# Attention with a squared-ReLU MLP behind it: q and k of six batches transposed by DMA instead of by TensorE

## The chip, the cores and the metric

One core of one Trainium2 chip runs the whole program. The metric is the device time of one execution in microseconds (us); a kernel is known by the median of its timed runs. The profile is of one further execution, whose own time stands beside its span. TensorE is PE in the profile (PEld its weight loads), VectorE is DVE, ScalarE is ACT, GpSimd is POOL and SyncE is SP; SP and POOL issue the DMAs.

## What is computed

```python
# q, k, v: (8, 12, 448, 64) fp32; w_in: (768, 2048); w_out: (2048, 768)
scores = (q @ k.transpose(0, 1, 3, 2)) / sqrt(64)
m = scores.max(-1, keepdims=True)
e = exp(scores - m)
attn = e / (e.sum(-1, keepdims=True) + exp(-m) + 1e-9)   # softmax with one more, empty, key
x = (attn @ v).transpose(0, 2, 1, 3).reshape(3584, 768)
out = maximum(x @ w_in, 0) ** 2 @ w_out                   # (3584, 768) fp32
```

The kernel leaves the maximum out: `exp(s) / (sum exp(s) + 1)` is the same quotient.

## The kernel before

**Pairs.** There are 8 batches of 12 heads. The unit of attention is a pair of heads, so 6 pairs a batch and 48 in all; one turn of the main loop (L251) works on one pair. The 448 tokens of a head lie on 112 partitions, four successive tokens to a partition (`P`, `RUN`), so the tokens fall into four groups `kk` of 112.

**q and k.** `load` (L78) brings q, k and v of a batch from DRAM through POOL's queue, which casts fp32 to fp16 on the way (tiles `qn`, `kn`, `vn`, two buffers each). For the first three pairs of batch 0 `load_raw` (L86) brings q and k as fp32 through SP's queue. The scores need the 64 dimensions of a head on partitions, so q and k are transposed: `regroup` (L102) has DVE copy three pairs at a time into `flatq` and `flatk`; `transposes` (L114) has PE make, for one pair, four transposes of `flatq` and four of `flatk` into one PSUM tile `mp`; DVE copies that to `qkt` (L121). In `qkt` the first head of the pair is on partitions 0 to 63, the second on 64 to 127.

**Scores and values.** `scores` (L124) makes, for one group `kk` of keys, two matmuls (one a head, 64 rows of the array each, 448 columns) into `sp`, and ACT takes the exponential into `et` (L129). `values` (L138) multiplies with v, `row_sums` (L144) adds up over the keys, ACT makes the reciprocal as `exp(-ln(z))`, and `normalise` (L154) writes the pair's columns of `xt`.

**MLP.** `mlp` (L161) is a generator: for a block of 384 (even batches) or 512 (odd batches) tokens it makes 16 times six matmuls with `win` into `mp` (L167), each followed on DVE by a maximum (L172) and a square (L174), and then 16 matmuls with `wout` for each half row of 128 tokens (L182), which ACT copies to `ot` (L186) and SP stores (L196). `drain` (L233) runs the generator for a share of its time at five places in a turn, so that the matmuls of the block of the batch before fill PE between the steps of attention. A batch's first turn still drains the end of the block before that one. The block of batch 7 runs alone at the end.

**Order.** Each engine works through its instructions in the order in which the program issues them. In a turn for pair i: scores of groups 0 and 1; transposes of pair i+1; MLP; scores of group 2; scores of group 3; values and row sums of pair i-1; MLP, with the three sums over `et` on DVE (L133, L136) between; normalise of pair i-1; and at the end of a turn with pr 1 the regroup of the same batch's pairs 3 to 5, with pr 4 that of the next batch's pairs 0 to 2. `mp` has two buffers in PSUM, shared by the transposes and the MLP; `sp` has two, `ot` two.

**Loads.** POOL's queue at the start: v of batch 0 (half), q and k of its pairs 3 to 5, the rest of v, three eighths of `win`, half of batch 1, three more eighths, the other half, the last two, four quarters of `wout`. Later a batch b+1 is loaded when turn (b, 0) is issued, as soon as the buffers are free.

Of the kernel before, what the change touches and what calls it, by code (L numbers as in the profile page):

```python
# [15 lines left out]
def kernel(  # L16
# [18 lines left out]
    P = S // RUN  # L35

# [34 lines left out]
    nats, flats, xts = {}, {}, {}  # L71

    def tiles_of(b):
        if b not in nats:
            nats[b] = {n: nat.tile([P, H, RUN, D], FP16, name=f"{n}n") for n in ("q", "k", "v")}
        return nats[b]

    def load(b, names, p0, p1):  # L78
        hs = slice(2 * p0, 2 * p1)
        for n in names:  # L80
            r = {"q": q_r, "k": k_r, "v": v_r}[n]
            nc.gpsimd.dma_start(out=tiles_of(b)[n][:, hs], in_=r[b, :, hs])  # L82

    raws = {}

    def load_raw(b, p0, p1):  # L86
        hs = slice(2 * p0, 2 * p1)
        for n, r in (("q", q_r), ("k", k_r)):
            t = raw.tile([P, 2 * (p1 - p0), RUN, D], FP32, name=f"{n}raw{p0}")
            nc.sync.dma_start(out=t, in_=r[b, :, hs])  # L90
            raws[n, b, p0] = t
# [10 lines left out]
    def regroup(b, p0, p1):  # L102
        hs = slice(2 * p0, 2 * p1)
        n = 2 * (p1 - p0)
        both = []
        for name in ("q", "k"):
            t = raws.pop((name, b, p0)) if (name, b, p0) in raws else nats[b][name][:, hs]
            f = flat.tile([P, RUN, H // 2, D], FP16, name=f"flat{name}")
            nc.vector.tensor_copy(f[:, :, 0:n, :], t.rearrange("p h t d -> p t h d"))  # L109
            both.append(f)  # L110
        for pr in range(p0, p1):
            flats[b, pr] = both, 2 * (pr - p0)

    def transposes(b, pr):  # L114
        both, h0 = flats.pop((b, pr))
        tp = m_psum.tile([128, 2, 512], FP16, name="mp")
        for i, t in enumerate(both):
            for s in range(RUN):
                nc.tensor.transpose(tp[:, i, P * s:P * s + P], t[:, s, h0:h0 + 2, :], ident[0:P, 0:P])  # L119
        qkt = qkt_pool.tile([128, 2, S], FP16, name="qkt")  # L120
        nc.vector.tensor_copy(qkt, tp[:, :, 0:S])  # L121
        return qkt

    def scores(qkt, et, kk):  # L124
        sp = s_psum.tile([P, 2, 512], FP32, name="sp")
        for h in range(2):
            r = slice(64 * h, 64 * h + 64)
            nc.tensor.matmul(sp[:, h, 0:S], qkt[r, 1, P * kk:P * kk + P], qkt[r, 0, :], start=True, stop=True)  # L128
# [8 lines left out]

    def values(b, pr, et, xp, kk):  # L138
        vn = nats[b]["v"]
        for h in range(2):  # L140
            nc.tensor.matmul(xp[64 * h:64 * h + 64, 0:S], vn[:, 2 * pr + h, kk, :], et[:, kk, h, :],  # L141
                             start=(kk == 0), stop=(kk == RUN - 1))

    def row_sums(es):  # L144
        zp = xz_psum.tile([128, 512], FP32, name="zp")
        for h in range(2):
            nc.tensor.matmul(zp[64 * h:64 * h + 64, 0:S], ones, es[:, 0, h, :], start=True, stop=True)  # L147
# [13 lines left out]
    def mlp(t0, n):  # L161
# [15 lines left out]
        for ts in range(n // 128):  # L177
# [13 lines left out]
            while c < end:  # L191
                b, t, p = c // S, c % S // P, c % P
                m = min(P - p, end - c)
                o = c + 128 - end
                rows = out[b * S:(b + 1) * S, :].rearrange("(p t) m -> t p m", t=RUN)
# [3 lines left out]


    load_raw(0, 0, 1)
    load_raw(0, 1, 3)
    load(0, "v", 0, 3)
    load(0, "qk", 3, 6)
    load(0, "v", 3, 6)
# [6 lines left out]
    for i in range(3):  # L212
        load_win(i, 8)
    load(1, "qkv", 0, 3)
# [114 lines left out]
```

## Time and profile before

| | us |
|---|---|
| median of 3 runs | 496.74 (496.45 to 499.69) |
| the profiled execution | 497.45 |
| its span, first to last instruction | 495.7 |
| PE busy in it | 448.1 |
| DVE busy in it | 280.8 |
| ACT busy in it | 244.2 |
| mean granted TensorE clock | 0.978 |

The span leaves 1.7 us of the execution around it. The turn of one batch after the other is seen at ACT's first reciprocal step (`lnz`, L150), once a pair: the second turns of batches 1 to 7 have it at 54.34, 109.13, 170.29, 225.08, 286.24, 341.07 and 403.13 us, and the last one stands at 446.09 us; from there to the end the block of batch 7 runs alone. In the views, a line of the timeline gives the start, the busy time, engine, line, tiles, shapes, how many are merged in it (x4), and in brackets how long the engine sat idle before it and what ended that. Busy time of PE includes the depth of its pipeline, so matmuls that are started 50 ns apart are shown as 200 ns each: the starts tell the pace.

### The profile page before, as it was taken

How to read it: one execution, taken by the hardware profiler on the slowest of the kernel's cores; microseconds unless marked ns; L12 is line 12 of the kernel's file. 1: busy time of each engine (PE TensorE's matmuls, PEld its weight loads, DVE VectorE, ACT ScalarE, POOL GpSimd, SP SyncE). 2: the span in 40 equal slices, each digit the busy share in tenths (PEclk: the TensorE clock that was granted, in tenths of full speed). 3: DMA queues.
4: the chain of work that ended last, by engine and by line, in shares of the span. 5: the costliest groups of instructions: out<-in, count | busy, mean ns of one | idle time of the engine just before them, and what ended most of it. 6: DMA issues, size and time to landing. Idle time of an engine off the chain costs nothing.

```text
span 495.7 us, 7052 instructions
## 1 busy us (share of the span) xinstructions
PE 448.1 (90%) x2912; PEld 221.9 (45%) x2912; DVE 280.8 (57%) x532; ACT 244.2 (49%) x345; POOL 35.5 (7%) x46
## 2 busy tenths in 40 slices
PE   1787789997999979997999988998999989999996
PEld 1333345543355534543355534553345544455453
DVE  2656766457853568457754466637684277635800
ACT  2688436663355635663365635565245663561011
POOL 6342100001000010001000010000000000000000
PEclk9998999999999989999999989999899998999999
DMA  9999990256112580144702545115001210021022
GB/s 184 197 197 206 205 184 7 65 87 86 26 33 65 88 110 3 33 68 66 99 1 64 79 79 75 34 32 89 0 2 33 63 33 0 1 65 32 1 62 67
DMA packets 45665, 34.97 MB, mean 71 GB/s; under 512 B 1600, under 2 KB 42048, under 8 KB 45632
## 3 DMA queue, kind: packets, MB, share of 16 engines
q0 software_dynamic: 39744, 22.12, 33.1%
q1 hardware_dynamic: 5888, 12.39, 8.5%
q8 instruction: 23, 0.38, 0.3%
q14 instruction: 10, 0.08, 0.0%
HBM read 45.61 MB, written 11.01 MB: 114 GB/s over the span
## 4 chain that ended last, share of the span: by engine, by line
PE 73%; DVE 20%; ACT 3%; DMA 2%; issue 1%; SPq 0%; ACTq 0%
PE mp L182 30%; PE mp L167 20%; PE xp L141 9%; PE sp L128 8%; DVE rt L172 6%; PE mp L119 4%; DVE es L133 4%; DVE g L174 4%; DMA kraw<-in_k_dram 2%; PE zp L147 2%; DVE xt L158 2%; ACT et L129 2%; DVE es L136 2%; DVE qkt L121 2%; DVE flatq L109 1%
## 5 line engine op out<-in xcount | busy, mean ns | idle before, releaser
L129 ACT ACTIVATE et<-sp 112x896 f16<-112x896 f32 x192 | 165.3, 913 | 167.9 <-PE sp L128 167.9
L167 PE MATMUL mp<-xt,win 128*128 128x384 f16 (+1 forms) x768 | 163.6, 363 | 6.5 <-DVE rt L172 3.5
L182 PE MATMUL mp<-wout,g 128*128 128x512 f16 (+1 forms) x896 | 153.9, 326 | 0.4
L167 PEld LDWEIGHTS <-win 128*128 128x128 f16 x768 | 74.5, 100 | 86.2 <-issue 27.9
L182 PEld LDWEIGHTS <-g 128*128 128x128 f16 x896 | 84.9, 98 | 61.0 <-issue 9.2
L172 DVE TENSOR_SCALAR rt<-mp 128x384 f16<-128x384 f32 (+1 forms) x128 | 79.6, 622 | 56.4 <-PE mp L167 53.2
L133 DVE TENSOR_TENSOR es<-et 112x896 f16<-112x896 f16 x96 | 59.1, 622 | 83.0 <-ACT et L129 82.8
L128 PE MATMUL sp<-qkt 64*112 64x448 f16 x384 | 62.3, 395 | 4.3 <-ACT et L129 3.6
L186 ACT ACTIVATE ot<-mp 128x512 f32<-128x512 f32 (+1 forms) x56 | 27.3, 487 | 72.8 <-PE mp L182 72.1
L174 DVE TENSOR_TENSOR g<-rt 128x384 f16<-128x384 f16 (+1 forms) x128 | 50.1, 392 | 4.4
L141 PE MATMUL xp<-et,vn 112*64 112x448 f16 x384 | 49.7, 377 | 0.0
L121 DVE COPY qkt<-mp 128x896 f16<-128x896 f16 x48 | 29.8, 621 | 32.3 <-PE mp L119 32.3
L119 PE MATMUL mp<-ident,flatq 112*128 112x112 f16 x192 | 19.0, 226 | 28.9 <-DVE flatq L109 20.6
L128 PEld LDWEIGHTS <-qkt 64*112 64x112 f16 x384 | 19.2, 130 | 42.3 <-issue 40.0
L150 ACT ACTIVATE lnz<-zp,one_b 128x448 f32<-128x448 f32 x48 | 30.7, 640 | 4.1 <-PE zp L147 4.1
L158 DVE TENSOR_TENSOR xt<-xp,rcp 128x448 f16<-128x448 f32 x48 | 29.7, 619 | 4.8 <-ACT rcp L151 4.4
L119 PEld LDWEIGHTS <-flatq 112*128 112x128 f16 x192 | 11.5, 102 | 46.3 <-DVE flatq L109 29.5
L136 DVE TENSOR_TENSOR es<-es 112x896 f16<-112x896 f16 x48 | 29.9, 623 | 1.2
L141 PEld LDWEIGHTS <-vn 112*64 112x64 f16 x384 | 17.5, 111 | 24.5 <-issue 18.2
L151 ACT ACTIVATE rcp<-lnz 128x448 f32<-128x448 f32 x48 | 27.7, 577 | 1.5
L82 POOL DMA_DIRECT2D vn<-in_v_dram x10 | 9.0, 898 | 220.5 <-PE zp L147 217.2
L119 PE MATMUL mp<-ident,flatk 112*128 112x112 f16 x192 | 19.1, 228 | 2.6 <-DVE flatk L109 2.0
(20 smaller groups left out, 83.3 us busy)
## 6 DMA issues: line engine op xcount, KB each, us to landing
qn<-in_q_dram POOLq DMA_DIRECT2D x6, 672.0 KB, 7.8
kn<-in_k_dram POOLq DMA_DIRECT2D x6, 672.0 KB, 10.5
vn<-in_v_dram POOLq DMA_DIRECT2D x6, 672.0 KB, 8.9
win<-in_moe_w_in_dram POOLq DMA_DIRECT2D x8, 384.0 KB, 15.4
wout<-in_moe_w_out_dram POOLq DMA_DIRECT2D x4, 768.0 KB, 18.9
out_dram<-ot SPq DMA_DIRECT2D x8, 336.0 KB, 2.8
out_dram<-ot SPq DMA_DIRECT2D x8, 288.0 KB, 2.7
out_dram<-ot SPq DMA_DIRECT2D x8, 240.0 KB, 2.8
```

The costliest lines, as they stand in the source:

```text
L119: nc.tensor.transpose(tp[:, i, P * s:P * s + P], t[:, s, h0:h0 + 2, :], ident[0:P, 0:P])
L121: nc.vector.tensor_copy(qkt, tp[:, :, 0:S])
L128: nc.tensor.matmul(sp[:, h, 0:S], qkt[r, 1, P * kk:P * kk + P], qkt[r, 0, :], start=True, stop=True)
L129: nc.scalar.activation(out=et[:, kk], in_=sp[:, :, 0:S], func=AF.Exp, scale=scale)
L133: nc.vector.tensor_add(es[:, c], et[:, cs.start], et[:, cs.start + 1])
L136: nc.vector.tensor_add(es[:, 0], es[:, 0], es[:, 1])
L141: nc.tensor.matmul(xp[64 * h:64 * h + 64, 0:S], vn[:, 2 * pr + h, kk, :], et[:, kk, h, :], start=(kk == 0), stop=(kk == RUN - 1))
L158: nc.vector.tensor_mul(xts[b // 2][:, pr, c:c + S], xp[:, 0:S], rcp)
L167: nc.tensor.matmul(hp[:, 0:n], win[:, dc, fb * 128:(fb + 1) * 128], xt[:, dc, x0:x0 + n], start=(dc == 0), stop=(dc == DCH - 1))
L172: nc.vector.tensor_scalar(out=rt[:, 0:n], in0=hp[:, 0:n], scalar1=0.0, scalar2=None, op0=ALU.max)
L174: nc.vector.tensor_mul(g[:, 0:n], rt[:, 0:n], rt[:, 0:n])
L182: nc.tensor.matmul(op[:, 0:n1 - n0], gt[fb][:, ts * 128:(ts + 1) * 128], wout[:, fb, n0:n1], start=(fb == 0), stop=(fb == NFFB - 1))
```

## The change

- Batches 0 and 1 (`ON_PE`) keep the transposes on PE. `regroup` copies one pair at a time and is called at the end of turn i for pair i+2. The loads of q and k come through POOL's queue but for the first pair, into tiles with one buffer each (`nat`), which batch 1's halves share with batch 0's; the order of POOL's first loads changes with it. The copy out of PSUM goes into a tile `qk` for the whole batch, with two buffers.
- For batches 2 to 7, `stage` has POOL's queue copy all of q and of k of a batch from DRAM to DRAM, cast to fp16 (688 KB each; it is called where the loads of q and k were). `transposed_loads` has SP's queue read these copies as rows of 128 values, two tokens of 64, and transpose them into `qk`: even tokens land on partitions 0 to 63, odd ones on 64 to 127. There are three of them for a batch: q, k, and k once more shifted by one token, so that each key is found on either half of the partitions. Nothing of these batches passes through `regroup`, `transposes` or the copy to `qkt`.
- `scores` for these batches makes four matmuls of 224 columns for a group of keys in place of two of 448: for each head, the even queries on rows 0 to 63 of the array and the odd ones on 64 to 127. The keys are read with a step of two. `sp` and `et` then hold even queries in one half and odd ones in the other; `of_head` picks a head's two pieces for `values` and `row_sums`, and the rows of the output are stored with a step of 2 in place of 4.

```diff
-    nat = ctx.enter_context(tc.tile_pool(name="nat", bufs=2))
-    raw = ctx.enter_context(tc.tile_pool(name="raw", bufs=1))
+    nat = ctx.enter_context(tc.tile_pool(name="nat", bufs=1))
+    v_pool = ctx.enter_context(tc.tile_pool(name="v", bufs=2))
...
-    qkt_pool = ctx.enter_context(tc.tile_pool(name="qkt", bufs=3))
+    qk_pool = ctx.enter_context(tc.tile_pool(name="qk", bufs=2))
...
+    def stage(b):
+        for n, t in (("q", q), ("k", k)):
+            st = nc.dram_tensor(f"stage_{n}{b}", (TOTAL,), FP16, kind="Internal").ap()
...
+                    nc.gpsimd.dma_start(out=st[x - lo:y - lo].rearrange("(r w) -> r w", w=w),
+                                        in_=src[x:y].rearrange("(r w) -> r w", w=w))
...
+    def transposed_loads(b):
+        qk = qks[b] = qk_pool.tile([128, 3, COLS], FP16, name="qk")
+        for i, n, x, c in ((0, "q", FRONT, H * S // 2), (1, "k", FRONT, H * S // 2), (2, "k", 0, COLS)):
+            nc.sync.dma_start(
+                out=qk[:, i, 0:c],
+                in_=stages[n, b][x:x + c * 2 * D].rearrange("(r c) -> r c", c=2 * D),
+                transpose=True,
+            )
...
-    def regroup(b, p0, p1):
+    def regroup(b, pr):
...
+            for h in range(2):
+                for odd in range(2):
+                    r = slice(64 * odd, 64 * odd + 64)
+                    c = (2 * pr + h) * (S // 2)
+                    kc = c + kk // 2
+                    which = 1
+                    if kk % 2 != odd:
+                        which = 2
+                        kc += kk % 2
+                    nc.tensor.matmul(sp[:, odd, h * (S // 2):(h + 1) * (S // 2)],
+                                     qk[r, which, kc:kc + 2 * P - 1:2], qk[r, 0, c:c + S // 2],
+                                     start=True, stop=True)
...
-    load_raw(0, 0, 1)
-    load_raw(0, 1, 3)
-    load(0, "v", 0, 3)
-    load(0, "qk", 3, 6)
-    load(0, "v", 3, 6)
+    load_natural(0, 0, 1)
+    load_natural(0, 1, 3)
+    load_v(0, 0, 3)
+    load_natural(0, 3, 6)
+    load_v(0, 3, 6)
...
             if pr == 0 and 0 < b and b + 1 < B:
-                load(b + 1, "qkv", 0, 6)
+                stage(b + 1)
+                load_v(b + 1, 0, NPAIR)
...
-            if i + 1 < NP:
-                qkts[i + 1] = transposes(*pairs[i + 1])
+            if i + 1 < NP and pairs[i + 1][0] in ON_PE:
+                transposes(*pairs[i + 1])
...
-            if pr == 1:
-                regroup(b, 3, 6)
-            if pr == 4 and b + 1 < B:
-                regroup(b + 1, 0, 3)
+            if i + 2 < NP and pairs[i + 2][0] in ON_PE:
+                regroup(*pairs[i + 2])
+            if pr == 2 and b + 1 < B and b + 1 not in ON_PE:
+                transposed_loads(b + 1)
```

PE, turn (3, 2), from the scores of groups 0 and 1 to the first matmuls of the MLP behind them, before (`sp` are scores, `mp` is PSUM for transposes and MLP; rows that only repeat are left out):

```order
L128 LDWEIGHTS qkt
L128 MATMUL sp<-qkt 112x448
L119 LDWEIGHTS flatq
L119 MATMUL mp<-ident,flatq 128x112
L119 LDWEIGHTS flatk
L119 MATMUL mp<-ident,flatk 128x112
L167 LDWEIGHTS win
L167 MATMUL mp<-xt,win 128x384
```

and in the change, from the matmul of the MLP ahead of them:

```order
L218 LDWEIGHTS win
L218 MATMUL mp<-xt,win 128x384
L171 LDWEIGHTS qk
L171 MATMUL sp<-qk 112x224
L218 LDWEIGHTS win
L218 MATMUL mp<-xt,win 128x384
```

Before there are four score matmuls there, then four transposes of `flatq` and four of `flatk`; in the change there are eight score matmuls and the MLP follows at once. PE has 2912 matmuls in both programs.

DVE, the end of turn (1, 1) and the start of turn (1, 2), before: the regroup of pairs 3 to 5 of batch 1 stands behind the last maximum, square and normalise of the turn, and directly ahead of the copy that follows the transposes of pair 3.

```order
L136 TENSOR_TENSOR es<-es 112x896
L172 TENSOR_SCALAR rt<-mp 128x384
L174 TENSOR_TENSOR g_611<-rt 128x384
L158 TENSOR_TENSOR xt<-xp,rcp 128x448
L109 COPY flatq<-qn 112x1536
L109 COPY flatk<-kn 112x1536
L121 COPY qkt<-mp 128x896
```

and the same place in the change:

```order
L181 TENSOR_TENSOR es<-es 112x896
L223 TENSOR_SCALAR rt<-mp 128x384
L225 TENSOR_TENSOR g_624<-rt 128x384
L209 TENSOR_TENSOR xt<-xp,rcp 128x448
L139 COPY flatq<-qn_143 112x512
L139 COPY flatk<-kn_145 112x512
L149 COPY qk<-mp 128x2x448
```

The two copies are of pair 3 alone there (512 columns in place of 1536), and the same rows come again a turn later for pair 4, and so at the end of every turn whose second next pair is of batch 0 or 1, where before they came at the end of two turns of a batch. From turn (1, 4) on no such rows are left on DVE.

SP's queue in the change, from the last stores of the block of batch 0 to the first of that of batch 1; in the program before, nothing stands between the two groups of stores:

```order
L249 DMA out_dram<-ot 80x768 [waits DMAHW1_49,Activation_49]
L249 DMA out_dram<-ot 48x768 [waits DMAHW2_49]
L129 DMA_TRANSPOSE qk<-stage_q 128x2688 [waits DMASW3_49,DMAHW3_49,DVE_49,PE_49]
L129 DMA_TRANSPOSE qk<-stage_k 128x2688 [waits DMAHW4_49,DMASW4_49]
L129 DMA_TRANSPOSE qk<-stage_k 128x2704 [waits DMAHW5_49]
L249 DMA out_dram<-ot 64x768 [waits DMAHW6_49,Activation_49]
```

The three transposing loads of batch 3 wait for the copies in DRAM (DMASW), for the buffer of `qk` (DVE, PE) and for the eighth DMA ahead of them (DMAHW); the stores of the next block stand behind them in SP's order.

More of the change, by code (lines that the diff above doesn't have):

```diff
@@ L99, in load_wout @@
         nc.gpsimd.dma_start(out=wout[:, i * w:(i + 1) * w, :], in_=wout_r[:, i * w:(i + 1) * w, :])
-    def regroup(b, p0, p1):
[L103 to L112, printed above, removed]
+    HSD = H * S * D
@@ L245 @@
     NP = len(pairs)
-    qkts, ets, ess = {}, {}, {}
-    regroup(0, 0, 1)
-    qkts[0] = transposes(*pairs[0])
-    regroup(0, 1, 3)
+    ets, ess = {}, {}
+    regroup(*pairs[0])
+    transposes(*pairs[0])
+    regroup(*pairs[1])
     share = 0.0
@@ L274 @@
                 values(*pairs[i - 1], ets[i - 1], xp, kk)
[L275 removed]
+            rcp = row_sums(pairs[i - 1][0], ess.pop(i - 1))
             ets.pop(i - 1)
```

115 lines of the change are left out of this document (71 added, 44 removed).

## The prediction

> **What bounds the kernel now.** The page comes first: PE is busy for 448.1 of 495.7 us, and DMA only in the first six of forty slices of 12.4 us.
>
> ```profile
> DMA  9999990256112580144702545115001210021022
> ...
> q0 software_dynamic: 39744, 22.12, 33.1%
> q1 hardware_dynamic: 5888, 12.39, 8.5%
> ```
>
> After some 74 us the DMA engines have room. So what counts is where PE, which works in order, stands still or does something that the change takes away. The list of waits, for PE alone:
>
> ```profile
> PE mp L119 <- DVE flatq L109: 20.6, 10, 2.2
> PE mp L119 <- POOL ident masks.py:199: 5.3, 1, 5.3
> PE sp L128 <- ACT et L129: 3.6, 7, 1.2
> PE mp L167 <- DVE rt L172: 3.5, 7, 0.6
> PE mp L119 <- DVE rt L172: 3.0, 7, 0.5
> PE mp L119 <- DVE flatk L109: 2.0, 1, 2.0
> PE mp L167 <- DVE qkt L121: 1.8, 7, 0.3
> ```
>
> The largest is that of the transposes for the regrouped q. The same list for the first 48 us holds three of the ten:
>
> ```profile
> PE mp L119 <- DVE flatq L109: 5.7, 3, 2.2
> ```
>
> so 14.9 us belong to seven waits of 2.1 us, one in each of batches 1 to 7. One of them in the timeline, at the start of turn (3, 2):
>
> ```profile
> 173.27 0.58 PE L128 MATMUL sp<-qkt 64*112 64x448 f16 x4
> 173.44 0.62 DVE L136 TENSOR_TENSOR es<-es 112x896 f16<-112x896 f16 x1
> ...
> 173.98 0.55 DVE L172 TENSOR_SCALAR rt<-mp 128x384 f16<-128x384 f32 x1
> 174.57 0.36 DVE L174 TENSOR_TENSOR g<-rt 128x384 f16<-128x384 f16 x1
> 174.84 0.62 DVE L158 TENSOR_TENSOR xt<-xp,rcp 128x448 f16<-128x448 f32 x1
> 175.38 0.55 DVE L109 COPY flatq<-qn 112x1536 f16<-112x1536 f16 x1
> ...
> 175.99 0.37 PE L119 MATMUL mp<-ident,flatq 112*128 112x112 f16 x4 [2.13 <-DVE flatq L109]
> ```
>
> PE has started its scores at 173.27 us and wants the transposes; DVE, without a gap, still has five instructions ahead of them, the last one the regroup. The stages show what follows such a wait (last three columns: granted clock, DMA share, GB/s):
>
> ```profile
> 54.34:109.13 54.79, 51.02 (x350) 25.72 (x348) 33.51 (x66) 29.79 (x44) 2.80 (x3) 0.97 0.69 103
> 109.13:170.29 61.16, 57.73 (x382) 28.44 (x381) 36.00 (x66) 30.82 (x46) 2.80 (x3) 1.00 0.36 58
> 170.29:225.08 54.79, 51.02 (x350) 25.65 (x348) 33.52 (x66) 29.79 (x43) 2.79 (x3) 0.97 0.38 63
> 286.24:341.07 54.83, 51.00 (x350) 25.67 (x348) 33.48 (x66) 29.79 (x44) 2.79 (x3) 0.97 0.37 61
> 341.07:403.13 62.06, 59.01 (x382) 28.97 (x381) 36.09 (x66) 30.82 (x46) 0.00 (x0) 0.97 0.10 28
> 403.13:446.09 42.96, 39.29 (x260) 19.80 (x258) 26.15 (x53) 21.15 (x32) 0.00 (x0) 0.96 0.06 19
> ```
>
> In five of these the granted clock was 0.96 or 0.97, which costs 3% of some 55 us, 1.6 us each.
>
> **The change part by part.** *Transposes.* In turn (4, 1) they stand like this:
>
> ```profile
> 253.11 0.58 PE L128 MATMUL sp<-qkt 64*112 64x448 f16 x4
> 253.63 0.37 PE L119 MATMUL mp<-ident,flatq 112*128 112x112 f16 x4
> 253.84 0.36 PE L119 MATMUL mp<-ident,flatk 112*128 112x112 f16 x4
> 254.03 3.31 PE L182 MATMUL mp<-wout,g 128*128 128x512 f16 x19
> ```
>
> Eight of them take PE from 253.63 to 254.03 us: 0.40 us. For the 36 pairs of batches 2 to 7 that is 14.5 us, all on PE's path.
>
> *The waits for flatq.* Six of the seven go, since those batches have no regroup: 6 x 2.1 = 12.6 us. *The clock.* Four of the five stages at 0.97 lie in batches that lose the wait; I take 4 x 1.5 = 6 us, bounds 0 (something else lowers it) and 6.4.
>
> *DVE.* What it no longer does:
>
> ```profile
> L121 DVE COPY qkt<-mp 128x896 f16<-128x896 f16 x48 | 29.8, 621 | 32.3 <-PE mp L119 32.3
> L109 DVE COPY flatk<-kn 112x1536 f16<-112x1536 f16 x15 | 8.3, 553 | 0.0
> L109 DVE COPY flatq<-qn 112x1536 f16<-112x1536 f16 x15 | 8.3, 551 | 0.0
> ```
>
> 36 copies of 0.62 us and four regroups of 0.55 us in each of six batches, 35 us of DVE. DVE does not set the end, so this counts only through PE's waits for it: the three rows of the list that name rt and qkt, 8.3 us. Those of L119 and of qkt go with the transposes, those of L167 for rt in part: 5 us, bounds 0 and 7.
>
> *Batches 0 and 1.* Here the flatq waits don't go, they multiply. The order of DVE keeps a regroup right ahead of the transposes that need it, now in every turn of these batches and not in two of six; each copies one pair and not three, so a wait of 2.1 us becomes one of perhaps 1.7. Some six more of them, less what the shorter copies save, is 5 us lost. At the start:
>
> ```profile
> 4.92 0.36 POOL masks.py:199 TENSOR_SCALAR_AFFINE_SELECT ident<-ident 128x128 f16<-128x128 f16 x1
> ...
> 11.96 0.69 DVE L109 CAST flatk<-kraw 112x1024 f16<-112x1024 f32 x1 [1.88 <-DMA kraw<-in_k_dram]
> ...
> 13.19 0.99 PE L128 MATMUL sp<-qkt 64*112 64x448 f16 x4
> ```
>
> Pair 0's last two score groups wait until 13.19 us behind the transposes of pair 1, which wait for a k of fp32 that DVE casts at 11.96 us. The new loads of pairs 1 and 2 are first in POOL's queue and write half the bytes; I put them 3 us earlier. The identity comes later, behind two more DMA issues of POOL, but within that wait. Net: 2 us lost, bounds 3 gained and 7 lost.
>
> *Scores.* Twice the instructions with half the columns. In the rows above four matmuls (two pairs, each pair side by side in the two halves of the array) take 253.11 to 253.63 us, 0.52 us; their columns at full clock, at the pace at which the transposes' 112 columns take 0.05 us, are 2 x 0.19. The other 0.14 us is either paid once a group of four, then eight matmuls cost the same; or it is paid by each pair, for weights that are loaded between two pairs on the same rows, then four pairs cost 0.14 us more. There are 72 such groups in 36 pairs: between 0 and 10 us lost. I take 5. The Trainium skill ("TensorE: Matmul & The Clock Gate", Part 3) says that a weight load overlaps a running matmul only when it is for other rows; by that the upper end would hold, and the sum would be 5 us higher. The rows here allow it, and don't show it.
>
> *The loads.* Staging moves the same reads through POOL's queue as the loads of q and k did, and adds the transposing loads on SP's. The program before has none, so their cost is bounded from the queues' rows. Each moves 2688 rows of 256 bytes, 688 KB. By q1's bytes (12.39 MB in 8.5% of 16 engines' 495.7 us: 18 bytes per ns and engine) one takes 2.3 us. By q0's packets (66 ns for one of 557 bytes), a packet a row, it takes 11 us; by q1's (115 ns for one of 2.1 KB) 19 us. The work of the next batch covers them:
>
> ```profile
> 96.73 0.58 PE L128 MATMUL sp<-qkt 64*112 64x448 f16 x4
> ...
> 390.15 0.59 PE L128 MATMUL sp<-qkt 64*112 64x448 f16 x4
> ```
>
> Batch 2 starts at 96.73 us. Its copies in DRAM stand behind the weights, where DMA is busy until 74 us, ahead of v, so done by about 68. That leaves 28 us for three loads, 9 us each; from then on SP may issue the next three when a batch starts, so they have a whole batch of 50 us. A reading of contiguous rows is nearest to the bytes; I take 6 us, which costs nothing. The stores behind them on SP come in the second half of a batch, later than 18 us. If the cover is gone, each late us of the three loads is a us of PE. The skill ("DMA: Bandwidth & Descriptors", Latency and other measured facts) gives a transposing DMA 261 GB/s, or 350 to 400 on contiguous data; as an estimate 1.7 to 2.6 us a load, and the sum the same. No run here shows it yet.
>
> **The sum.** 14.5 + 12.6 + 6 + 5 - 2 - 5 = 31 us less than the profiled execution's 497.45: 466. That execution lies 0.7 us over the median of 496.74, so 465.5 against the median. With half of the way to each bound, 459 to 476; with all of them at once 453 to 487.
>
> **The rivals.** *First batch late.* If a row is a packet of 66 ns, three loads take 33 us, more where v of batch 2 and the copies of batch 3 share the engines (10 us). Then batch 2 starts near 110 and not 96 us, and later batches are on time: 465.5 + 14 = 480. For it: no row shows 256-byte rows any faster. Against it: q1 moves bytes well.
>
> *The wait moves.* PE waited for flatq because DVE was behind by five instructions; without it PE may wait for rt two matmul groups later. Then a third of 12.6 comes, no clock, 2 of the 5: 14.5 + 4 + 2 - 2 - 5 = 13.5, so 483. Against it: DVE is busy for 33.5 of 54.8 us in a batch and loses 6 x 0.62 + 2.2 = 5.9 of them.
>
> *Weights in the scores.* Keys are read with a step of two. If the loads of the weights become slower by that, each of two more pairs a group shows one whole:
>
> ```profile
> L128 PEld LDWEIGHTS <-qkt 64*112 64x112 f16 x384 | 19.2, 130 | 42.3 <-issue 40.0 <-DVE qkt L121 1.5 <-DVE es L133 0.7
> ```
>
> 72 x 2 x 0.13 = 19 us in place of 5: 479.
>
> *Slower: the transposing loads set the pace.* Three of them must fit in a batch. With T us each, batch 2 starts at 68 + 3T, batch 7 another 15T later, and from there to the end it takes the 105.5 us of today less some 8, and 1.8 around the span: 167 + 18T. At T = 18.3 that is today's time; at the 19 us of q1's packets it is 509, and a T twice that gives 850. For it: that row is of the very queue that issues them. Against it: those packets carry eight times a row's bytes.
>
> **How the numbers follow.** Forecast 0.58, first batch late 0.10, the wait moves 0.12, weights 0.08, slower 0.09; 0.03 for no change, where several small losses meet. A measurement of this kernel tells about 1% from no change. Faster: 0.87 (0.58 + 0.10 + 0.12 + 0.08, less a little for their tails); same 0.04; slower 0.09. The range goes from the low end with all bounds to the case in which the wait moves: 453 to 483.
>
> **What would show it.** Right: the waits of PE name flatq in batches 0 and 1 alone, up to ten times; the stages of batches 2 to 6 are some 5 to 7 us shorter each, at a clock of 1.00; the group of eight score matmuls takes 0.52 to 0.66 us; the transposing loads land within 9 us each, and no score waits for a DMA. Wrong: scores that wait for `qk` at each batch's first turn (the loads are too slow), a PE wait for rt of 2 us at turns (b, 2) (the wait moved), score groups beyond 0.7 us, or stores held up so that ACT waits for `ot`.

## The result, and the profile after

| | us |
|---|---|
| before, median of 4 runs | 498.22 (496.45 to 501.19) |
| the change, median of 4 runs | 469.00 (466.40 to 472.74) |
| the change to before, 95% interval | 0.941 (0.932 to 0.951) |
| the profiled execution of the change, and its span | 466.42, 464.7 |

The sum of the prediction said 466 for the profiled execution, and that took 466.42; for the median it said 465.5, and the median is 469.00. The four runs fall into two pairs, 466.4 and some 472, with granted clocks of 0.974 and 0.982 against 0.960 and 0.962; the profile is of the first pair. Of the runs told of below, two of the four of e8 (its profiled one too) and three of the four of e5 lay more than 1.5% above the fastest of the same kernel, so they enter no ratio.

The page of the change, rows 2 and 3: clock and DMA in slices of 11.6 us, and the two queues.

```profile
PEclk9995689999999999999999999999999999999999
DMA  9999999977931299227951299228801100020022
...
q0 software_dynamic: 25056, 22.63, 32.3%
q1 hardware_dynamic: 53824, 23.88, 28.2%
```

After the fifth slice the row shows no long half clock again (what it leaves out of the start is told below); q1 moves twice the bytes that it did before. The list of waits, PE alone, complete, and below it the row for flatq in the first two stages apart (0 to 58.44 us, then to 114.19):

```profile
PE mp L146 <- DVE flatq L139: 14.1, 10, 1.9
PE mp L146 <- POOL ident masks.py:199: 6.6, 1, 6.6
PE mp L218 <- DVE rt L223: 5.1, 13, 0.6
PE sp L159 <- DVE qk L149: 0.7, 1, 0.7
PE sp L159 <- ACT et L174: 0.6, 2, 0.4
PE mp L218 <- DVE qk L149: 0.4, 1, 0.4
```

```profile
PE mp L146 <- DVE flatq L139: 9.4, 7, 1.7
```

```profile
PE mp L146 <- DVE flatq L139: 4.7, 3, 1.9
```

The two make up the 14.1: no wait for flatq is left in batches 2 to 7, there are ten in batches 0 and 1, and no row names a DMA. Now the stages, from one batch's second turn (ACT's `lnz`, L201) to the next one's. The columns are the window, its length, the busy time of PE, PEld, DVE, ACT and POOL with counts, the granted clock, the DMA share and GB/s.

```profile
0.00:58.44 58.44, 41.11 (x224) 16.79 (x225) 28.25 (x60) 35.92 (x45) 22.62 (x35) 0.82 1.29 194
58.44:114.19 55.75, 49.78 (x342) 25.23 (x340) 31.17 (x65) 29.81 (x43) 1.95 (x3) 0.97 1.06 118
114.19:169.94 55.75, 55.17 (x382) 28.38 (x381) 30.31 (x56) 30.87 (x46) 1.95 (x3) 1.00 0.54 105
169.94:218.28 48.34, 46.92 (x350) 25.04 (x348) 27.88 (x56) 29.82 (x44) 1.95 (x3) 1.00 0.58 109
218.28:274.01 55.73, 55.15 (x382) 28.36 (x381) 30.30 (x56) 30.85 (x45) 3.89 (x7) 1.00 0.59 105
...
416.17:464.70 48.53, 44.78 (x247) 23.96 (x245) 18.50 (x33) 6.12 (x12) 0.00 (x0) 1.00 0.13 41
```

Taken stage by stage against before, in us:

| stage | before | after | difference |
|---|---|---|---|
| start to batch 1's second turn | 54.34 | 58.44 | +4.1 |
| batch 1 | 54.79 | 55.75 | +1.0 |
| batches 2, 4, 6 | 61.16, 61.16, 62.06 | 55.75, 55.73, 55.74 | -17.2 |
| batches 3, 5 | 54.79, 54.83 | 48.34, 48.35 | -12.9 |
| batch 7 | 42.96 | 38.07 | -4.9 |
| the last block | 49.61 | 48.53 | -1.1 |
| span | 495.7 | 464.7 | -31.0 |

So 35 us come from the six changed batches, 5 go back in the two unchanged ones, and the last block gives 1. In a stage of 512 tokens PE is busy for 55.15 of 55.73 us: nothing but its own work is left there.

What became of the three things the prediction was unsure of. First the scores, a group of the change in PE's timeline:

```profile
236.61 0.59 PE L171 MATMUL sp<-qk 64*112 64x224 f16 x8
237.13 0.95 PE L192 MATMUL xp<-et,vn 112*64 112x448 f16 x8
```

Eight matmuls of 224 columns take 236.61 to 237.13, 0.52 us, as four of 448 did. Then the transposing loads of batch 2, in SP's issue queue and in the windows around them:

```profile
61.68 28.45 SPq L129 DMA_TRANSPOSE qk<-stage_q  x1
90.19 6.94 SPq L129 DMA_TRANSPOSE qk<-stage_k  x2
```

```profile
65.00:90.00 25.00, 21.21 (x130) 10.17 (x131) 16.60 (x38) 9.20 (x13) 0.00 (x0) 0.93 1.34 78
90.00:100.00 10.00, 10.00 (x75) 5.29 (x72) 2.47 (x5) 7.74 (x12) 0.00 (x0) 1.00 1.15 218
```

By the trace they landed at 93.9, 96.6 and 99.2 us: the first 32 us after its issue, the others some 2.7 us apart. While v of batch 2 and the copies of batch 3 were running beside the first one (until 90.2 us), all queues together moved 78 GB/s with the DMA engines busy; without them, 218. Batch 2's first scores started at 102.69 us. So in this execution the loads came in time, by 3.5 us. Last the start:

```profile
6.63 0.53 PE L146 MATMUL mp<-ident,flatq 112*128 112x112 f16 x4 [6.63 <-POOL ident masks.py:199]
...
10.04 1.27 PE L159 MATMUL sp<-qk 64*112 64x448 f16 x4
...
20.39 0.55 PE L146 MATMUL mp<-ident,flatq 112*128 112x112 f16 x4 [1.27 <-DVE flatq L139]
...
26.82 0.55 PE L146 MATMUL mp<-ident,flatq 112*128 112x112 f16 x4 [1.33 <-DVE flatq L139]
```

Pair 0's last scores start at 10.04 us, 3 us earlier than before, as predicted; after that, turn follows turn at 6.43 us (26.82 - 20.39), each with a wait for flatq; and four transposes are shown as 0.55 us, where before, in batch 4, they were shown as 0.37: PE works at half its pace here.

### The profile page after: what moved, and what is told of

Its sections match the earlier page's. It is cut to its first block, busy times and chain, and to the rows that moved or that the text cites. A ratio compares the mean times of both kernels' runs of the same rounds, so it can differ in the third digit from the quotient of the medians.

```text
span 464.7 us, 7026 instructions
## 1 busy us (share of the span) xinstructions
PE 431.7 (93%) x2912; PEld 220.7 (47%) x2912; DVE 247.8 (53%) x486; ACT 245.2 (53%) x345; POOL 33.3 (7%) x52
## 4 chain that ended last, share of the span: by engine, by line
PE 76%; DVE 19%; ACT 2%; POOL 1%; issue 1%; ACTq 0%; POOLq 0%
PE mp L233 32%; PE mp L218 20%; PE xp L192 10%; PE sp L171 7%; DVE rt L223 7%; DVE es L178 4%; DVE g L225 3%; PE sp L159 2%; PE zp L198 2%; DVE xt L209 2%; PE mp L146 2%; DVE es L181 2%; ACT lnz L201 1%; ACT rcp L202 1%; DVE flatq L139 1%
## 5 line engine op out<-in xcount | busy, mean ns | idle before, releaser
L218 PE MATMUL mp<-xt,win 128*128 128x384 f16 (+1 forms) x768 | 160.2, 358 | 6.9 <-DVE rt L223 5.1
L233 PEld LDWEIGHTS <-g 128*128 128x128 f16 x896 | 84.3, 98 | 63.6 <-issue 10.8
L218 PEld LDWEIGHTS <-win 128*128 128x128 f16 x768 | 72.7, 99 | 86.1 <-issue 26.1
L192 PE MATMUL xp<-et,vn 112*64 112x448 f16 x384 | 50.9, 384 | 0.0
L171 PE MATMUL sp<-qk 64*112 64x224 f16 x576 | 42.8, 268 | 0.0
L171 PEld LDWEIGHTS <-qk 64*112 64x112 f16 x576 | 26.9, 127 | 25.4 <-issue 25.4
L201 ACT ACTIVATE lnz<-zp,one_b 128x448 f32<-128x448 f32 x48 | 30.7, 639 | 5.0 <-PE zp L198 5.0
L146 PE MATMUL mp<-ident,flatq 112*128 112x112 f16 x48 | 5.9, 267 | 20.7 <-DVE flatq L139 14.1
L159 PE MATMUL sp<-qk 64*112 64x448 f16 x96 | 21.6, 504 | 1.3 <-DVE qk L149 0.7
L198 PE MATMUL zp<-es,ones 112*64 112x448 f16 x96 | 18.5, 381 | 0.0
L146 PEld LDWEIGHTS <-flatq 112*128 112x128 f16 x48 | 3.5, 119 | 27.1 <-DVE flatq L139 24.1
## 6 DMA issues: line engine op xcount, KB each, us to landing
stage_q<-in_q_dram POOLq DMA_DIRECT2D x5, 676.0 KB, 13.7
```

Source lines behind the costliest of these rows:

```text
L171: nc.tensor.matmul(sp[:, odd, h * (S // 2):(h + 1) * (S // 2)], qk[r, which, kc:kc + 2 * P - 1:2], qk[r, 0, c:c + S // 2], start=True, sto ...
L201: nc.scalar.activation(out=lnz, in_=zp[:, 0:S], func=AF.Ln, bias=one_b)
L218: nc.tensor.matmul(hp[:, 0:n], win[:, dc, fb * 128:(fb + 1) * 128], xt[:, dc, x0:x0 + n], start=(dc == 0), stop=(dc == DCH - 1))
L233: nc.tensor.matmul(op[:, 0:n1 - n0], gt[fb][:, ts * 128:(ts + 1) * 128], wout[:, fb, n0:n1], start=(fb == 0), stop=(fb == NFFB - 1))
```

## The experiments

All times are of four runs; the ratio is to the kernel before, measured beside it, with its 95% interval. Each edit is made to the change, but e1 (to the kernel before), e6 and e10 (to e2) and e11 (to e6).

| run | median us (lowest to highest) | ratio |
|---|---|---|
| e1, before with its regroups a turn earlier | 480.68 (479.15 to 482.31) | 0.967 (0.962 to 0.971) |
| e2, regroup a turn earlier in the change | 471.80 (469.97 to 472.55) | 0.948 (0.944 to 0.952) |
| e4, all batches on PE | 523.03 (522.97 to 524.71) | 1.053 (1.048 to 1.058) |
| e5, every transposing load twice | 477.70 (470.58 to 478.82) | none |
| e6, e2 with the loads apart from the copies | 451.61 (450.11 to 453.26) | 0.906 (0.899 to 0.913) |
| e7, that move alone | 466.59 (466.35 to 467.01) | 0.937 (0.930 to 0.944) |
| e8, DVE's work put back | 485.67 (479.05 to 490.66) | 0.964 (0.954 to 0.974) |
| e9, PE's transposes put back | 482.95 (482.34 to 483.31) | 0.969 (0.964 to 0.975) |
| e10, e2 with copies in small pieces | 451.57 (450.06 to 455.02) | 0.905 (0.899 to 0.910) |
| e11, e6 with the identity first | 450.30 (449.60 to 450.70) | 0.901 (0.897 to 0.904) |

**e1: what the wait alone is worth.** In the kernel before, only the place of the regroups is moved, so that DVE copies a turn ahead of the transposes.

```diff
-            if pr == 1:
+            if pr == 0:
                 regroup(b, 3, 6)
-            if pr == 4 and b + 1 < B:
+            if pr == 3 and b + 1 < B:
                 regroup(b + 1, 0, 3)
```

> The kernel before, with both regroups called one turn earlier (end of turn 0 and of turn 3 in place of 1 and 4) and nothing else changed; PE still makes every transpose. Theory (the waits for flatq are an accident of order, and the drops of the clock come from them): the seven waits of 2.1 us and the five stages at 0.97 go, 14.9 + 8 us, so about 475 us (470 to 480), and PE's list of waits names flatq in the first 48 us alone. Rival (the wait is DVE's backlog and only moves): PE waits for rt or for the copy to qkt in its place, 485 to 494 us.

Measured 480.68, 17 us less. The waits of PE in e1:

```profile
PE mp L167 <- DVE qkt L121: 8.0, 18, 1.1
PE mp L119 <- DVE rt L172: 8.0, 14, 0.7
...
PE mp L119 <- DVE flatq L109: 3.3, 1, 3.3
```

The 2.1 us waits are gone, and with them the clock's drops on record, but for one that begins 1.1 us before the end. But qkt has grown from 1.8 to 8.0 us and rt at L119 from 3.0 to 8.0: 11 us came back as waits for DVE's next results. Over batches 2 to 7 the stages are 10.8 us shorter than before (61.16 became 60.09, 54.79 became 52.68). Neither range holds: 480.68 lies between the two, and the waits show why, since both mechanisms are in it.

**e4: batches 2 to 7 as batches 0 and 1.** All batches take the path of natural loads, regroups pair by pair and transposes on PE.

```diff
-    ON_PE = (0, 1)
+    ON_PE = tuple(range(B))
...
-                stage(b + 1)
+                load_natural(b + 1, 0, 3)
+                load_natural(b + 1, 3, 6)
```

> The changed kernel with all eight batches on PE, so the pair by pair part of the change alone: no staging, no transposing loads, q and k of batches 2 to 7 loaded by halves as in batch 1, 448 columns in the scores. Theory (a regroup right ahead of the transposes that need it costs a wait in each turn in which DVE is behind): in each of six batches three waits of 1.6 us in place of one of 2.1, some clock, and batches 0 and 1 as in the change: 505 to 520 us, slower than before. Rival (smaller copies make up for the number of them): 495 to 503 us, the same as before.

```profile
PE mp L146 <- DVE flatq L139: 47.7, 34, 1.9
```

523.03, 5% slower than before: the rest of the change (a regroup a pair, one `qk` tile, other loads) is a loss by itself, made of that wait. A stage of 512 tokens takes 65.1 us where it took 61.2, and the trace has eight stretches of 3.4 us at half clock after batch 1's second turn. The gain is that of the DMA transposes, not of what was rebuilt around them, and batches 0 and 1 of the change pay this price.

**e9 and e8: what of the gain is PE's, what DVE's.** e9 puts eight transposes a turn back on PE in batches 2 to 7, whose result nobody uses; e8 puts the copies back on DVE (one of 1792 columns a turn for the copy to `qkt`, two of 1536 twice a batch for the regroups), also unused.

```diff
...
+                    for s in range(2 * RUN):
+                        nc.tensor.transpose(tp[:, s // RUN, P * (s % RUN):P * (s % RUN) + P], wout[0:P, s, 0:128],
+                                            ident[0:P, 0:P])
```

```diff
...
+                    nc.vector.tensor_copy(spare, wout.rearrange("p c n -> p (c n)")[:, 0:1792])
...
+            elif i + 2 < NP and pr in (1, 4):
+                for _ in range(2):
+                    spare = spare_pool.tile([128, 1792], FP16, name="spare")
+                    nc.vector.tensor_copy(spare[:, 0:1536], wout.rearrange("p c n -> p (c n)")[:, 0:1536])
```

> The changed kernel with eight PE transposes put back into each turn of batches 2 to 7 (of parts of wout, into the PSUM tile that they had; nobody reads it, and DVE copies nothing). Theory (they cost their 0.40 us of PE each time, 14.5 us in all): 480 to 486 us. Rival (PE has idle time in a turn that takes them in): 475 us or less.

> The changed kernel with DVE's work of batches 2 to 7 put back without its use: in each turn one copy of 1792 columns out of wout into a spare tile at the place of the copy to qkt (some 0.62 us), and two of 1536 columns at the places of the regroups. No PE transposes, and nothing waits for these copies but what is behind them on DVE. Theory (DVE's work itself made PE wait for rt: of the 4.3 us by which a batch of the change is shorter than one with an early regroup, 1.9 are DVE's): 1.5 to 2.5 us more in each of six batches, 476 to 484 us, with rt back in PE's list. Rival (DVE is beside the path in these batches): 466 to 472 us.

A stage of 512 tokens of e9, then one of e8 at full clock, and the wait that grew in e8:

```profile
224.14:282.92 58.78, 57.32 (x430) 30.86 (x429) 30.68 (x56) 30.82 (x45) 3.89 (x7) 1.00 0.53 98
```

```profile
232.16:290.12 57.96, 55.31 (x382) 28.33 (x381) 35.74 (x66) 30.83 (x45) 4.36 (x7) 1.00 0.56 101
```

```profile
PE mp L219 <- DVE rt L224: 18.7, 22, 2.0
```

e9: 58.78 for 55.73 and 50.97 for 48.35 us; over the six batches 15.7 us, in which PE is busy 11.5 us longer and idle 4.2 us longer (its waits for rt are 10.2 us in all in place of 5.1). e8: 57.96 for 55.73, so 2.2 us a batch, though PE has not one instruction more (382 matmuls in both); it waits for rt 18.7 us in all in place of 5.1, and six of these waits, of 1.86 to 1.98 us, stand one to a batch, behind the first scores of its third turn, where the waits for flatq stood before. The profiled execution of e8 took 490.66 us, so only the stage at full clock is read; those of batches 3 and 5 have a drop of the clock, and PE waits 5.7 us for batch 2's loads. Both theories hold: PE's part is worth about what its instructions take, and DVE's part some 13 us (six times 2.2; 479.05 and 481.14, the two runs that enter the ratio, against 466.4).

**e5: are the loads on the path?** Each transposing load is issued twice.

```diff
-        for i, n, x, c in ((0, "q", FRONT, H * S // 2), (1, "k", FRONT, H * S // 2), (2, "k", 0, COLS)):
+        loads = ((0, "q", FRONT, H * S // 2), (1, "k", FRONT, H * S // 2), (2, "k", 0, COLS))
+        for i, n, x, c in loads + loads:
```

> The changed kernel, in which each batch's three transposing loads are issued twice, the second three over the first (six loads, same data). Theory (alone a load takes 2.6 us, a batch covers them, and only those of batch 2, which land 3.5 us before they are needed, have little room): batch 2 starts some 5 us late, the rest is covered: 467 to 475 us. Rival one (a load costs the 11 us of 2688 packets of 66 ns): batch 2 is 30 us late: 490 us or more. Rival two (the loads are not covered at all): 8 us more in each of six batches: 510 us or more.

```profile
PE sp L172 <- DMA qk<-stage_k: 2.1, 1, 2.1
```

The profiled run took 470.58 and has one wait for `qk`, of 2.1 us, ahead of batch 2; from its second turn on all stages are those of the change (55.74 and 48.35). The other three runs took 477.7 to 478.8 at clocks of 0.96 to 0.97 (the profiled one 0.984) and left no trace, so what lengthened them stays open; they lie above the expected 467 to 475. In the one that can be read, six loads a batch still hide but for these 2.1 us, and the rivals in which the loads set the pace, with 490 us or more, are out.

**e2: the waits of batches 0 and 1.** The regroup is called for pair i+3 in place of i+2, with three buffers, and once more ahead of the loop.

```diff
-    flat = ctx.enter_context(tc.tile_pool(name="flat", bufs=2))
+    flat = ctx.enter_context(tc.tile_pool(name="flat", bufs=3))
...
+    regroup(*pairs[2])
...
-            if i + 2 < NP and pairs[i + 2][0] in ON_PE:
-                regroup(*pairs[i + 2])
+            if i + 3 < NP and pairs[i + 3][0] in ON_PE:
+                regroup(*pairs[i + 3])
```

> The changed kernel, with the regroup of a pair of batches 0 and 1 one turn earlier (pair i+3 at the end of turn i, three buffers for it). Theory (the 5 us lost in batches 0 and 1 are the multiplied waits for flatq, and the 20 us at half clock that follow them): some 12 of the 14.1 us of flatq waits go, and with them part of the half clock: 450 to 458 us against 466 to 472 for the change. Rival (in batches 0 and 1 PE is held by the clock and by ACT whatever DVE does): only batch 1's 4.7 us go, 461 us or more.

```profile
PE sp L171 <- DMA qk<-stage_k: 17.9, 2, 14.2
```

```profile
100.94 0.43 PE L171 MATMUL sp<-qk 64*112 64x224 f16 x1 [14.23 <-DMA qk<-stage_k]
105.01 0.99 PE L171 MATMUL sp<-qk 64*112 64x224 f16 x7 [3.64 <-DMA qk<-stage_k]
```

The forecast failed: 471.8 in place of 450 to 458. The waits for flatq are gone and batch 1's second turn came at 46.56 us, not 58.44. But batch 2 then wanted its q and k at 86.7 us, and the loads landed at 98.2, 100.9 and 105.0: 17.9 us of the gain turned into a wait for them, in which a half clock of 20.5 us begins (89.6 us). The rival that the prediction called "first batch late" is real, and in the change only the slow batches 0 and 1 hid it.

**e6 and e7: why the loads were late.** v is issued ahead of the copies, and all batches share one DRAM buffer for q and one for k, so that the copies of batch 3 have to wait until batch 2's loads have read theirs. e6 is e2 with that, e7 the change with that.

```diff
-            st = nc.dram_tensor(f"stage_{n}{b}", (TOTAL,), FP16, kind="Internal").ap()
-            stages[n, b] = st
+            if n not in stages:
+                stages[n] = nc.dram_tensor(f"stage_{n}", (TOTAL,), FP16, kind="Internal").ap()
+            st = stages[n, b] = stages[n]
...
+                load_v(b + 1, 0, NPAIR)
                 stage(b + 1)
-                load_v(b + 1, 0, NPAIR)
```

> The kernel with the lead of two turns, whose batch 2 waited 17.9 us for its transposing loads, with two things moved in addition: v of the next batch is loaded ahead of the copies to DRAM, and all batches use one copy of q and one of k in DRAM, so that the copies for batch b+1 wait until the transposing loads of batch b have read theirs. Theory (those loads are slow only while casting DMAs run beside them; alone they take 2.7 us each, so batch 2's are there by some 75 us): no wait for qk, no clock drop behind it, and the 12 us that batches 0 and 1 gained with the lead stay: 450 to 456 us. Rival (the loads are slow for a reason of their own, or the copies now come too late in every batch): 465 us or more, with waits for qk in several batches.

> The changed kernel with the same two moves and without the lead. Theory (in the change no score waits for a transposing load, so making them faster gains nothing): the same as the change, 465 to 473 us, though the three loads of batch 2 land 2 to 4 us after one another and some 20 us earlier. Rival (the overlap costs the changed kernel time that the waits do not show): 460 us or less.

SP's queue and the window from 65 to 90 us in e6:

```profile
63.95 3.60 SPq L130 DMA_TRANSPOSE qk<-stage_q  x1
67.60 7.48 SPq L130 DMA_TRANSPOSE qk<-stage_k  x2
```

```profile
65.00:90.00 25.00, 24.25 (x167) 12.28 (x165) 12.97 (x27) 14.26 (x22) 0.00 (x0) 1.00 0.63 112
```

The three landed at 69.8, 74.4 and 77.1 us, and e6 takes 451.61: PE waits neither for flatq nor for a DMA in it. In e7 they land just as early (71.0, 73.9, 76.5, where the change has 93.9 to 99.2), and the time, 466.59, is that of the change's profiled execution, 466.42. So the lateness cost that execution nothing, and costs e2 20 us.

What is left open is the other two runs of the change. All four of e7 lie between 466.35 and 467.01 us, one of them at a clock of 0.960; of the change, two took 471.58 and 472.74. And the room that batch 2's loads have is not the same each time: the last one landed at 99.2 us in the profile of the change, at 100.4 in that of e9, and at 108.3 in that of e8, where PE waited for it. That the change's two longer runs waited for these loads is likely by this; no trace of them was kept, so it is not shown.

**e10: which copies hold the loads up.** e2 in its old order, but with the copies to DRAM cut into pieces of 32768 values.

```diff
-            for x, y in ((lo, lo + m), (lo + m, hi)):
+            step = 32 * 1024
+            cuts = [(x, min(x + step, lo + m)) for x in range(lo, lo + m, step)] + [(lo + m, hi)]
+            for x, y in cuts:
```

> The kernel with the lead of two turns (batch 2 waited 17.9 us for its transposing loads there), with each copy to DRAM cut into pieces of 32768 elements, issued one by one: descriptors of 2048 elements in place of 10816, in the old order, so that casting DMAs still run beside the transposing loads of batch 2. Theory one (what holds the transposing loads up are the long descriptors of the copies, 21 KB each, some 1 us apiece): the first of them lands some 15 us after its issue or less in place of 37, no wait for qk worth naming, 450 to 458 us. Theory two (any casting DMA beside them does it): the wait for qk stays above 10 us, 466 us or more.

Packets, MB and share of each queue from 65 to 90 us, in the change and then in e10:

```profile
q1 hardware_dynamic: 1131, 0.29, 75.6%
q0 software_dynamic: 660, 1.67, 58.5%
```

```profile
q0 software_dynamic: 2225, 2.38, 63.1%
q1 hardware_dynamic: 7967, 2.53, 55.0%
```

On average, a row of 256 bytes took 75.6% of 16 engines' 25 us over 1131 packets, 267 ns, in the change, and 55.0% over 7967, 28 ns, in e10 (there some packets of the stores among them). By the packets in the trace, the copies of the change move 21,632 bytes at a time, in 2.0 us each on average (1.6 in the median); those of e10 4,096, in 0.39 us. The average of 267 ns hides two kinds: half of the 1131 rows took 26 ns or less, and 165 took over 0.5 us, 1.66 us on average, about as long as one long packet; these make up 273 of the 302 us. e10 takes 451.57 us, and PE waits for no transposing load, though POOL's queue moves more in these 25 us (2.38 MB for 1.67): casting copies beside the loads are not the trouble by themselves, their long packets are. (The pieces are also issued one by one; that was not tested apart from their length.) Even so the small ones slow the loads: the first one landed 12.5 us after its issue, against 5.9 in e6.

**e11: the identity first.** e6 with `make_identity` ahead of POOL's first loads.

```diff
+    ident = consts.tile([128, 128], FP16)
+    make_identity(nc, ident)
     load_natural(0, 0, 1)
...
-    ident = consts.tile([128, 128], FP16)
-    make_identity(nc, ident)
```

> The kernel with the lead of two turns and no overlap (451.6 us), with the identity made ahead of POOL's first DMAs. PE's first wait is 6.8 us for the identity, while both regrouped tiles are there at 4.8 us; POOL's loads start some 0.7 us later. Theory (the first pair is on the path): PE starts at about 5 us, 1 to 2 us less: 449 to 451 us. Rival (batch 0 is held by its loads): 451 to 453 us, no change that can be measured.

```profile
4.43 0.56 PE L147 MATMUL mp<-ident,flatq 112*128 112x112 f16 x4 [4.43 <-DVE flatq L140]
```

The first transposes start at 4.43 us in place of some 6.8, and wait for q instead. 450.30 against 451.61, each measured beside other runs of the kernel before, and with ranges that overlap: a gain of 1 to 2 us is likely, not shown. It is the lowest median here.

## Why the prediction was right, point by point

**What bounds the kernel, and the transposes (14.5 us).** Right. e9 puts them back and pays 15.7 us, 11.5 of it in PE's busy time.

**The waits for flatq, the clock and DVE (12.6 + 6 + 5 = 23.6 us).** The sum is nearly right, its split is not. Batches 2 to 7 are 35.0 us shorter; without the 14.5 of the transposes that is 20.5, and what the scores cost, 0.6, comes on top: 21.1. But the 18.6 us put down to flatq and the clock were not to be had by taking that wait away: e1 does so and gains 10.8 us in these batches, because PE then waits for rt and qkt. The wait was the place where DVE's lateness showed, not its cause. What kept the other waits from growing in the change is that DVE has less to do, 30.31 us in 56 instructions in the stage of batch 2 where it had 36.00 in 66; e8 gives it back and loses 13 us, with no wait for flatq in these batches, and a wait of 1.9 us for rt in its place. The rival "the wait moves" was the right mechanism for a change that moves the wait, and wrong for one that removes the work behind it, for the very reason that the prediction set against it.

The clock itself went as said: 1.00 in all stages of batches 2 to 7. In before, stretches of 3.4 us at half clock began at 60.6, 176.7, 292.7, 347.3 and 408.8 us, each within a microsecond of the end of a wait of 2.13 us; the two other such waits, which end at 115.58 and 231.54 us, have none. In e4 they stand by waits of 1.7 and 1.9 us, in e7 a wait of 1.86 us has none; and in e1, where no wait after the start is over 1.1 us, there is none until 1.1 us before the end. That such a wait can bring the drop is what these runs suggest; no run here lowers the clock by itself.

The 1.1 us of the last block are a thing that the prediction did not have. They are not the clock's: PE is busy for 44.78 us in that block in both kernels. They lie behind its last matmul, from where it is 4.8 us to the end of the span before and 3.7 now. The rows of the output are stored with a step of 2 and not 4, and so one store stands there in place of two; in e1 and e4, which have the step of 4 and two stores, it is 4.8 and 4.9 us, in the others, with one store, 3.7 to 4.1.

**Batches 0 and 1 (-2 us, measured -5.1).** The step that was mis-sized, though inside its bounds (+3 to -7). The three us at the start came; the count of the waits, "up to ten", came too. But the loss was priced by the waits alone, 1.7 us each less what shorter copies save, and the clock was put at nothing in these two batches. What grew in the first stage is PE's own time. The first stage before, and in e2:

```profile
0.00:54.34 54.34, 36.54 (x224) 15.26 (x225) 27.55 (x50) 35.13 (x45) 21.48 (x31) 0.97 1.28 197
```

```profile
0.00:46.56 46.56, 32.31 (x224) 14.91 (x225) 28.59 (x62) 34.35 (x45) 22.69 (x35) 0.96 1.31 188
```

With the same 224 matmuls PE is busy for 36.54 us before and for 41.11 in the change, 4.6 us more, while its idle time is 17.8 and 17.3 us. In e2 it is busy for 32.31 and idle for 14.25 us: of the 11.9 us by which e2 is earlier than the change, 8.8 are PE's pace and 3.1 its idle time, though waits of 9.4 us are gone from the list.

The pace shows in the transposes: four of them take 0.37 us, and 0.55 within the half clock on record (34.7 to 55.2 us in the change). By that measure PE works at half pace from its first transposes to 28 us and from 40 to 44 us before, and in the change to 55 us, but for a few us ahead of 34.7. The records of the clock miss much of this. In e7 they say 1.00 for the first 58 us, and its transposes say half pace throughout; it is busy for 43.06 us in that stage:

```profile
26.96 0.56 PE L147 MATMUL mp<-ident,flatq 112*128 112x112 f16 x4 [1.33 <-DVE flatq L140]
...
52.72 0.56 PE L147 MATMUL mp<-ident,flatq 112*128 112x112 f16 x4 [1.33 <-DVE flatq L140]
```

The wait itself is worth less than its length. In e6, without it, the turns look like this:

```profile
18.19 0.56 PE L147 MATMUL mp<-ident,flatq 112*128 112x112 f16 x4
...
23.65 0.39 PE L147 MATMUL mp<-ident,flatq 112*128 112x112 f16 x4
...
27.75 0.37 PE L147 MATMUL mp<-ident,flatq 112*128 112x112 f16 x4
...
32.68 0.56 PE L147 MATMUL mp<-ident,flatq 112*128 112x112 f16 x4
...
38.20 0.56 PE L147 MATMUL mp<-ident,flatq 112*128 112x112 f16 x4
```

5.5 us from turn to turn at half pace (18.19 to 23.65, 32.68 to 38.20) and 4.1 at full pace (23.65 to 27.75), against 6.43 in the change at half pace: a wait shown as 1.3 us makes the turn 0.9 us longer, and the pace makes it 1.4 us longer. In the six traces with these waits in all turns of batch 0 (the change, e4, e5, e7, e8, e9) half pace lasts to between 53 and 57 us, in the five that have none after the start (e1, e2, e6, e10, e11) to between 28 and 44. That PE's idle time at the waits keeps the pace low is likely and not shown, since no run changes the one without the other.

**The scores (-5 us, measured less than -1).** Also mis-sized, on the other side. A group of eight takes 0.52 us (0.525 in the median of the groups after 120 us, where four of 448 took 0.517; 72 times the difference is 0.6 us), so what lies behind the columns is paid once a group, not for each pair, and keys read with a step of two cost nothing. By the rule of the Trainium skill ("TensorE: Matmul & The Clock Gate", Part 3), that a weight load overlaps only a matmul on other rows, the cost would have been 10 us. The trace does not agree with the rule as it stands: here the two halves of the array alternate, and the four pairs of a group start 0.143, 0.096 and 0.095 us apart, the last two about the 0.095 us that 224 columns take at the transposes' pace, so that the load for a pair on the same rows is hidden behind the pair before.

**The sum.** That 466 met 466.42 is luck. The waits, the clock and DVE gave 2.5 us less than forecast (21.1 for 23.6) and batches 0 and 1 lost 3.1 more; the scores cost 4.4 less, and the last store gave 1.1 that nobody had counted.

**The loads (6 us each, free if within 9).** Right that they cost nothing in the profiled execution; 6 us each was too much where nothing runs beside them, and too little beside the copies. Alone those of batch 2 come 2.65 us apart, 688 KB in that time being 260 GB/s; the bound by bytes (2.3 us) was the good one. The Trainium skill ("DMA: Bandwidth & Descriptors", Latency and other measured facts) gives 261 GB/s, or 350 to 400 on contiguous data; the lower figure agrees, and no run here shows the higher. But "the transposing loads land within 9 us each", one of the marks set for being right, failed for the first load of every batch: from issue to landing it took 32.2 us in batch 2 and 10.8 to 17.3 in batches 3 to 7, where e7, with the copies out of the way, has 5.9 to 7.3. In batches 3 to 7 there was a batch of room for it. In batch 2 there was not: the prediction had named the cause as an aside (v and the copies of batch 3 sharing the engines) and gave it 10 us. It was hidden because SP issued the loads at 61.68 and not 68 us, and because the mis-sized batches 0 and 1 put batch 2's start to 102.69 us. At the 96.73 us that the prediction reckoned with, the last load, at 99.2 us, would have been 2.5 us late; that is luck too.

## What to carry to other kernels

A wait in the profile is priced twice: by removing the wait alone (e1: 17 us, with 11 us of new waits in its train) and by removing the work behind it (the change); here the second was worth more, and the list of waits doesn't tell them apart. The length of a wait is not its price: 1.3 us of it were 0.9 us of a turn at the same pace of PE. So compare turns at the same pace, and read the pace from like instructions (0.37 or 0.56 us for four transposes), not from the clock on record alone, which said 1.00 for e7. And when a part of the kernel gets faster, look at what lands next with little room (3.5 us for the loads of batch 2): e2 took 14 us of waits away and won nothing until e6 moved the transfers apart.

## What the runs showed of the hardware

- Transposing loads beside casting copies with packets of 21.6 KB: 267 ns on average for a row of 256 bytes (26 ns in the median, with 165 of 1131 rows at 1.66 us), 72 to 78 GB/s for all queues together (e2 and the change, 65 to 90 us), with the engines shown as busy. That such a row stands behind one long packet is read from the two lengths, not shown by itself. Beside packets of 4 KB: 28 ns, 198 GB/s. From 90 to 100 us in the change, without the copies:

```profile
q1 hardware_dynamic: 7199, 2.17, 114.6%
```

114.6% of 16 engines' 10 us over 7199 packets is 25 ns each, the stores' among them. A row of 256 bytes thus takes less than half of the 66 ns that a packet of 557 bytes took in the queue before, and ten times that on average beside the long packets.

- The half clock on record comes in lengths of 3.4 us (before), 6.8 (e5), 13.7 (e6), 20.5 (the change) and 34.1 us (e9), whole multiples of 3.41. It leaves out part of the start: in e7 the record says 1.00 up to 58 us, in the change up to 34.7 us, while four transposes are shown as 0.53 to 0.56 us from the first ones on (in the change up to those at 26.82 us). So the change, e9 and e7, with 0.82, 0.71 and 1.00 on record for the first stage, reach batch 1's second turn within 2 us of each other (58.44, 59.02 and 59.97 us): by the transposes all three work at half pace for nearly all of that time.
